# Channel products by batch pairs, the first as seven products of halves, weights and gates kept in DRAM, two mixes moved

## The chip, the cores and the metric

The kernel runs on one core of a Trainium2 chip, in one launch. The metric is the device time of that core in microseconds; the median of three runs of the kernel before is 1045.92 (1045.71 to 1046.95).

## What is computed

Four batches of 448 positions and 768 channels pass through three blocks: attention with a sigmoid in place of the softmax (12 heads of 64), a mixing block with a low-rank mix over positions and a channel MLP of 3072, and a gated block with a causal convolution of five taps.

```python
def _attn_ref(q, k, v):
    scores = scale * np.matmul(q, k.transpose(0, 1, 3, 2)) - np.log(S)
    attn = 1.0 / (1.0 + np.exp(-scores))
    return np.matmul(attn, v)
def _moe_ref(x, U, V, w_ch1, w_ch2):
    u = x + (x.transpose(0, 2, 1) @ U @ V).transpose(0, 2, 1)
    return u + np.maximum(u @ w_ch1, 0.0) @ w_ch2
def _moe2_ref(x, w_val, conv_w, w_out):
    gate = 1.0 / (1.0 + np.exp(-gate_pre))   # gate_pre: causal convolution of x, 5 taps
    return (gate * (x @ w_val) @ w_out)
```

The weights arrive as float64 and are taken as pairs of 32-bit words.

## The kernel before

Activations lie with channels on the 128 partitions and the 448 positions along the row: a batch is 6 blocks of 128 channels (`KC`), the hidden layer 24 blocks (`NF`). `xs` holds x of all four batches and is updated in place.

**Numbers.** A float64 weight becomes a float32 in `unpack` (L83): one ScalarE instruction (L88) and two VectorE instructions (L89, L90) on a half of 384 columns. Each float32 operand of the channel products is then cut into a high part (ScalarE copy, L77) and a low part (VectorE subtraction, L79), and `mm3` (L200) does three matmuls per block of 128 x 128 x 448: high x high, high x low, low x high (L202 to L204).

**Order.** All engines work in the order in which the program issues instructions to them; the order is written out by hand. `flush` (L67) issues the parts put off in `deferred`: one part of a chain of small steps goes out per product, so that a step finds its input done. `load_half` (L145) and `prep_half` (L155) bring in, unpack and split one half of a weight block; they are called between products, in the order that `plan` (L130) lays down. Three buffers hold raw weights, 11 (`WS`) hold split halves, 32 (`OPS`) hold split activations of [128, 2, 448]. All weight loads go through SP's queue.

**Stages.** In attention (`attention_phase`, L547) 12 rounds handle two pairs of heads each; the mixes of batches 0 to 2 (`mix_units`, L382: transposes, projection, back-projection, add to x, split) are slipped in between, and the first three weight halves. The mix of batch 3 is done by `main_phase` (L620) between the first channel products. The channel stage then goes through 12 groups of two hidden blocks. `ch1` (L457) is the first product for one hidden block and one batch: 6 x 3 matmuls into one PSUM bank, a Relu on ScalarE (L460) and the low part on VectorE (L461). `ch2` (L466) is the second product for one output block and one batch: 2 x 3 matmuls, and an add onto x (L473). All four batches go through each group, so each weight is split once. While this goes on, the halves of the two last weight matrices are unpacked, split and stored to DRAM (`stash`), and fetched twice at the end.

**End.** For each half of the batches `val` (L518) is x @ w_val, multiplied by the gate from `gate_steps` (L490: a scaled copy on ScalarE, L499, four multiply-adds on VectorE, L502, a sigmoid on ScalarE, L515); `fin` (L529) is the last product, copied out on ScalarE and stored.

PSUM has 8 banks; `bank` (L543) hands them out in turn.

## Time and profile before

| | |
|---|---|
| median of three runs | 1045.92 us |
| the profiled execution | 1045.58 us |
| its span, first to last instruction | 1043.8 us |
| TensorE matmul busy | 1035.0 us, 99% |
| VectorE busy | 580.0 us, 56% |
| ScalarE busy | 328.8 us, 32% |
| moved by DMA | 98.97 MB, mean 95 GB/s |

Attention fills the span up to about 155 us, the channel products reach to about 865 us, then come the value and the output products. In the profile PE is TensorE's matmul, PEld its weight load, DVE VectorE, ACT ScalarE, SP the engine that issues most transfers; L202 is a line of the kernel. Matmuls overlap in the pipeline, so the pace of a stretch is its time divided by its matmuls, not the mean duration of one.

### The profile page before, as it was taken

The page shows a single profiled execution, that of the slowest core. Times are in us where ns is not written, and L with a number is a line of the kernel's source. Part 1 is how long each engine was busy: PE and PEld are TensorE (multiplying, and loading weights), DVE is VectorE, ACT ScalarE, POOL GpSimd, SP SyncE. Part 2 cuts the span into 40 slices and gives each one's busy share as a digit, 9 for nine tenths or more (in the row PEclk, how much of TensorE's full clock was granted, in tenths as well). Part 3 has the DMA queues.
Part 4 walks back from the last instruction along what each step waited for, and adds up shares of the span by engine and source line. Part 5 has one row for each costly group of instructions (what it writes and reads, how often), then busy time and mean ns, then how long its engine had stood idle before and what let it go on. Part 6 is the DMA issues. An engine that isn't in the chain of part 4 may idle for free.

```text
span 1043.8 us, 13756 instructions
## 1 busy us (share of the span) xinstructions
PE 1035.0 (99%) x5505; PEld 895.0 (86%) x5505; DVE 580.0 (56%) x1057; ACT 328.8 (32%) x562; POOL 1.0 (0%) x6
## 2 busy tenths in 40 slices
PE   9999999999999999999999999999999999999998
PEld 5555547999999999999999999999999999999997
DVE  5455665766556464656456464646455678992100
ACT  6656664223141312213040312223130443231211
POOL 0000000000000000000000000000000000000000
PEclk9999999999999999999999999999999999999999
DMA  7444441233133322314141322314142014332441
GB/s 190 122 107 107 106 112 54 76 122 121 61 113 100 87 80 76 106 46 134 30 114 56 91 79 73 106 56 127 31 131 79 3 61 136 106 110 74 162 173 71
DMA packets 47616, 98.97 MB, mean 95 GB/s; under 512 B 10832, under 2 KB 19984, under 8 KB 47552
## 3 DMA queue, kind: packets, MB, share of 16 engines
q1 hardware_dynamic: 47280, 97.75, 31.5%
q8 instruction: 43, 0.70, 0.3%
q10 hardware_dynamic: 224, 0.23, 0.1%
q14 instruction: 21, 0.17, 0.0%
q0 software_dynamic: 48, 0.11, 0.0%
HBM read 83.13 MB, written 14.94 MB: 94 GB/s over the span
## 4 chain that ended last, share of the span: by engine, by line
PE 98%; DVE 1%; ACT 1%; DMA 0%; SPq 0%; issue 0%; DVEq 0%
PE ch L202 22%; PE ch L204 22%; PE ch L203 22%; PE av L310 5%; PE sc L279 4%; PE fin L204 3%; PE val L204 3%; PE val L202 3%; PE fin L202 3%; PE val L203 3%; PE fin L203 3%; PE tr L391 1%; PE av L323 1%; PE sl L295 1%; PE pp L413 1%; PE h L434 0%
## 5 line engine op out<-in xcount | busy, mean ns | idle before, releaser
L473 DVE TENSOR_TENSOR xs<-ch,xs 128x448 f32<-128x448 f32 x288 | 177.7, 622 | 101.8 <-PE ch L204 101.0
L203 PE MATMUL ch<-h,w 128*128 128x448 f32 x576 | 210.6, 366 | 0.0
L204 PE MATMUL ch<-h,w 128*128 128x448 f32 x576 | 210.6, 366 | 0.0
L202 PE MATMUL ch<-h,w 128*128 128x448 f32 x576 | 210.6, 366 | 0.0
L202 PE MATMUL ch<-u,w 128*128 128x448 f32 x570 | 208.7, 366 | 1.3 <-DVE xs L438 1.3
L203 PE MATMUL ch<-u,w 128*128 128x448 f32 x570 | 208.4, 366 | 0.0
L204 PE MATMUL ch<-u,w 128*128 128x448 f32 x570 | 208.4, 366 | 0.0
L77 ACT ACTIVATE w<-x 128x384 fp32r<-128x384 f32 x120 | 63.0, 525 | 353.8 <-DVE x L90 353.8
L461 DVE SCALAR_TENSOR_TENSOR h<-ch,h 128x448 fp32r<-128x448 f32 x95 | 59.3, 624 | 178.3 <-ACT h L460 178.3
L202 PEld LDWEIGHTS ch<-u,w 128*128 128x128 f32 x570 | 107.2, 188 | 10.4 <-DVE xs L438 1.7
L203 PEld LDWEIGHTS ch<-h,w 128*128 128x128 f32 x576 | 108.3, 188 | 8.4
L204 PEld LDWEIGHTS ch<-h,w 128*128 128x128 f32 x576 | 108.3, 188 | 8.4
L202 PEld LDWEIGHTS ch<-h,w 128*128 128x128 f32 x576 | 108.3, 188 | 8.4
L204 PEld LDWEIGHTS ch<-u,w 128*128 128x128 f32 x570 | 107.2, 188 | 8.4
L203 PEld LDWEIGHTS ch<-u,w 128*128 128x128 f32 x570 | 107.2, 188 | 8.3
L460 ACT ACTIVATE h<-ch 128x448 fp32r<-128x448 f32 x95 | 51.6, 543 | 144.2 <-PE ch L204 144.2
L90 DVE SCALAR_TENSOR_TENSOR x<-a,x 128x384 uint32<-128x384 uint32 x120 | 67.1, 559 | 14.0 <-ACT a L88 1.8
L79 DVE TENSOR_TENSOR w<-x,w 128x384 fp32r<-128x384 f32 x120 | 66.2, 552 | 4.7 <-ACT w L77 2.6
L267 ACT ACTIVATE a<-sc,bias 128x896 f32<-128x896 f32 x72 | 67.1, 1006 | 5.3 <-PE sc L279 5.3
L88 ACT ACTIVATE a<-raw 128x384 f32<-128x384 f32 x120 | 64.9, 541 | 0.3 <-DMA raw<-in_w 0.3
L310 PE MATMUL av<-a,vr 128*64 128x448 f32 x288 | 59.4, 548 | 0.0
L279 PEld LDWEIGHTS sc<-ks 64*128 64x128 f32 x432 | 37.9, 185 | 20.6 <-issue 4.6
(83 smaller groups left out, 988.2 us busy)
## 6 DMA issues: line engine op xcount, KB each, us to landing
raw<-in_w SPq DMA_DIRECT2D x96, 384.0 KB, 3.1
f<-s SPq DMA_DIRECT2D x48, 384.0 KB, 3.3
kq<-in_kq SPq DMA_DIRECT2D x47, 224.0 KB, 3.7
s<-w SPq DMA_DIRECT2D x24, 384.0 KB, 2.7
out_t<-o SPq DMA_DIRECT2D x11, 448.0 KB, 2.8
raw<-in_wval SPq DMA_DIRECT2D x12, 384.0 KB, 3.1
raw<-in_wout SPq DMA_DIRECT2D x12, 384.0 KB, 3.0
vr<-in_va SPq DMA_DIRECT2D x24, 168.0 KB, 3.7
```

The lines of the kernel that those rows point to most:

```text
L77: nc.scalar.activation(hi, raw, AF.Copy)
L79: deferred.append(lambda: nc.vector.tensor_sub(lo, raw, f32(hi)))
L88: nc.scalar.activation(a, f32(high), AF.Prelu, scale=2.0 ** -112, alpha=-(2.0 ** 32))
L90: nc.vector.scalar_tensor_tensor(x, a.bitcast(U32), 3, x, op0=ALU.logical_shift_left, op1=ALU.bitwise_or)
L202: mm(ps, wk[:, 0], x[:, 0], start=start, stop=False)
L203: mm(ps, wk[:, 0], x[:, 1], start=False, stop=False)
L204: mm(ps, wk[:, 1], x[:, 0], start=False, stop=stop)
L267: nc.scalar.activation(a[:, :, :], ps[:, :, :S], AF.Sigmoid, bias=bias, scale=1.0 / math.sqrt(D))
L279: mm(ps[:, h, :S].rearrange("p (c s) -> p c s", c=NSC), ks[r, tk, 0, c], ks[r, tq, 1, :, :SC], start=t == 0, stop=t == 2,)
L310: mm(att["ps"][D * h:D * h + D, :S], vr[:, h, c], a[:, h], start=c == 0, stop=False,)
L461: nc.vector.scalar_tensor_tensor(t[:, 1], ps, 0.0, f32(t[:, 0]), op0=ALU.max, op1=ALU.subtract)
L473: nc.vector.tensor_add(y, ps[:, :S], y)
```

## The change

- **Batch pairs.** The channel stage runs twice, for batches 0 and 1 (p = 0) and then for 2 and 3 (p = 1). Within a pair it goes in 6 quads of four hidden blocks: two chains, then the second product of the quad.
- **First product.** `chain` handles two hidden blocks, two batches and the two halves of the 6 input blocks as a 2 x 2 by 2 x 2 product in seven products (Strassen's, in Winograd's form). Each is a `part` of 3 x 3 = 9 matmuls. Sums of weights (S1 to S4: four VectorE instructions per chain) and of activations (T1 to T4: `u_sums`) are formed beforehand; results are put together by copies of PSUM on ScalarE (p1, u2, p5), further accumulation onto the bank already copied, and three VectorE adds.
- **Second product.** `ch2` does three output blocks at once for one batch, over the quad's four hidden blocks: 4 parts of 9 matmuls, then three adds onto x. There are 144 adds in place of 288.
- **Weights.** For p = 0 each half is unpacked from float64 as before, and the float32 value is also stored to DRAM (`keep`); for p = 1 it is loaded from there, and the sums and splits are made again. Ten buffers hold split halves.
- **Order.** `plan` writes one list of jobs; `step`, called after each part, issues one of them (`pump`) unless that needs more than the ten buffers. `weight` issues jobs at once where a product needs a form that is not there yet. Where the quads of p = 1 are planned, four stashed halves of the last matrices and, in quads 1 to 3, the gates of batches 0 and 1 (now stored to DRAM and fetched) stand among the jobs, in front of the second product's weights.
- **Moves.** The mixes of batches 2 and 3 go out between chains and second products of quads 0 to 2 of p = 0. Attention's last rounds take the sums of activations for p = 0 and the first eight jobs. The sums for p = 1 (`rush`) are issued two per part beside the last second products of p = 0.

The core of the diff:

```diff
...
-OPS = 32
-WS = 11
+OPS = 30
+WS = 10
+RAWS = 3
...
+    def pump(force=False):
+        if jobs and (force or live[0] + jobs[0][0] <= WS):
+            jobs.pop(0)[1]()
+
+    def done_with():
+        live[0] -= len(spent)
+        spent.clear()
+
+    def wtile(name):
+        if "w" not in pools:
+            return operand(name)[:, :, :HQ]
+        live[0] += 1
+        return pools["w"].tile([P, 2, HQ], F32R, tag="w", name=name)[:, :, :]
+
...
+    def keep(slot, part, x):
+
+        if slot not in kept:
+            kept[slot] = pools["kept"].tile([P, 2, HQ], F32, tag="kept", name="k_%s%d" % slot)
+        nc.sync.dma_start(kept[slot][:, part], x)
+
+    def in_two(x, t, then=None):
+
+        nc.scalar.activation(t[:, 0], x, AF.Copy)
+
+        def low():
+            nc.vector.tensor_sub(t[:, 1], x, f32(t[:, 0]))
+            if then:
+                then()
+
+        deferred.append(low)
...
+        def half(i, j):
+            key = ("w1", c + i, j)
+            x[i, j] = to_x(key)
+            deferred.append(lambda: keep(("w1", c + i), j, x[i, j]))
...
+        def first():
+            if p:
+                got(0)
+            put("A11", x[0, 0])
+            put("A12", x[0, 1])
+
+        def sums():
+            if p:
+                got(1)
+            s1 = pools["x"].tile([P, HQ], U32, tag="x", name=f"s1_{p}_{c}")[:, :]
+            x["s1"] = f32(s1)
+            nc.vector.tensor_add(x["s1"], x[1, 0], x[1, 1])
+            nc.vector.tensor_sub(x[1, 0], x[0, 0], x[1, 0])
+
+        def differences():
+            nc.vector.tensor_sub(x[0, 0], x["s1"], x[0, 0])
+            nc.vector.tensor_sub(x[0, 1], x[0, 1], x[0, 0])
+
+        def third():
+            put("S2", x[0, 0])
+            put("S1", x["s1"])
+
+        def fourth():
+            put("S3", x[1, 0])
+            put("S4", x[0, 1], load_next if p else None)
+
+        def fifth():
+            put("A22", x[1, 1], load_next if p else None)
+
+        unpacks = [[lambda i=i, j=j: half(i, j) for j in range(2)] if not p else [] for i in range(2)]
+        if p:
+            loads.extend(("x", "w1", c + i, p) for i in range(2))
+        else:
+            loads.extend(("w1", c + i, j) for i in range(2) for j in range(2))
+        todo = [(0, f) for f in unpacks[0]] + [(2, first)] + [(0, f) for f in unpacks[1]]
+        return todo + [(0, sums), (0, differences), (2, third), (2, fourth), (1, fifth)]
...
+        def again(n, half):
+            def job():
+                a = loaded.pop(("x", f"h{half}_", n // 2, p))
+                ts = [wtile(f"w2_{p}_{n + i}_{half}") for i in range(2)]
+
+                def done(i):
+                    forms[p, n + i, half] = ts[i]
+                    if i:
+                        load_next()
+
+                for i in range(2):
+                    in_two(a[:, i], ts[i], lambda i=i: done(i))
+            return job
+
         for half in range(2):
-            t = pools["w"].tile([P, 2, HQ], F32R, tag="w", name=f"f{n}_{p}_{half}")[:, :, :]
-            nc.sync.dma_start(f32(t), stash[2 * n + half][:, :, :])
+            for n in range(QUAD * q, QUAD * q + QUAD, 2 if p else 1):
+                if p:
+                    loads.append(("x", f"h{half}_", n // 2, p))
+                    out.append((2, again(n, half)))
+                else:
+                    loads.append(("w2", n, half))
+                    out.append((1, fresh(n, half)))
+        return out
...
+    def weight(*key):
+        while key not in forms:
+            if deferred:
+                flush()
+            else:
+                pump(True)
+        return forms[key]
...
+    def u_sums(p, k):
+
+        u = {(i, j): x_of(halves[p][i], k + KH * j) for i in range(2) for j in range(2)}
+        t = {}
+
...
+        def first():
+            both("T1", "T2")
+            difference("T1", u[1, 0], u[0, 0])
+            difference("T2", u[1, 1], t["T1"])
+
+        def second():
+            both("T4", "T3")
+            difference("T4", u[0, 1], t["T2"])
+            deferred.append(lambda: (cut("T2"), cut("T1")))
+
+        def third():
+            difference("T3", u[1, 1], u[1, 0])
+            deferred.append(lambda: (cut("T3"), cut("T4")))
+
+        return [first, second, third]
...
+        def part(ps, ws, ts, start=False):
+            done_with()
+            flush()
+            w = weight(p, c, ws)
+            if (p, c, ws) not in early:
+                spent.append(1)
+            for k in range(KH):
+                mm3(ps, w, k, us[(p, ts), k], start and k == 0, k == KH - 1, skip_group_check=True)
...
+        def finish(i, j, x, other):
+            nc.vector.tensor_add(x, x, other)
+            deferred.append(lambda: relu(i, j, x))
+
+        x, z = (bank(f"{k}_{p}_{c}")[:, :S] for k in "xz")
+        part(x, "A11", "B11", True)
+        p1 = copy("p1", x)
+        step()
+        y = bank(f"y_{p}_{c}")[:, :S]
+        part(y, "A12", "B21", True)
+        deferred.append(lambda: finish(0, 0, p1, y))
+        step()
+        part(x, "S2", "T2")
+        u2 = copy("u2", x)
+        step()
+        part(z, "S1", "T1", True)
+        p5 = copy("p5", z)
+        step()
+        part(x, "S3", "T3")
+        finish(1, 1, p5, x)
+        step()
+        part(z, "S4", "B22")
+        deferred.append(lambda: finish(0, 1, u2, z))
+        step()
+        part(x, "A22", "T4")
+        relu(1, 0, x)
+        step()
+
+    def ch2(p, q, b, half, step, then=None):
+        ps = [bank(f"ch2_{p}_{q}_{b}_{half}_{j}")[:, :S] for j in range(KH)]
+        for i in range(QUAD):
+            done_with()
+            flush()
+            w = weight(p, QUAD * q + i, half)
+            if b == halves[p][-1]:
+                spent.append(1)
+            h = hs[p, QUAD * q + i, b]
+            for j in range(KH):
...
+                step()
+
+        def add():
+            for j in range(KH):
+                m = half * KH + j
+                y = x_of(b, m)
+                nc.vector.tensor_add(y, ps[j], y)
+                if then:
+                    then(b, m)
+
+        deferred.append(add)
...
+        def add(k):
+            nc.vector.scalar_tensor_tensor(t[0], y(k), tap(k), t[0], op0=ALU.mult, op1=ALU.add)
+
+        def first():
+            t.append(operand(f"g{bs[0]}_{m}", F32)[:, :, :])
+            nc.scalar.activation(t[0], y(0), AF.Copy, scale=tap(0))
+            deferred.append(lambda: add(1))
+
+        def second():
+            add(2)
+            add(3)
+
+        def third():
+            add(4)
+            deferred.append(sigmoid)
+
+        def sigmoid():
+            nc.scalar.activation(t[0], t[0], AF.Sigmoid)
+            deferred.append(put)
+
+        def put():
+            gates_kept[m] = pools["gates"].tile([P, 2, S], F32, tag="gates", name=f"gk{m}")
+            nc.sync.dma_start(gates_kept[m][:, :, :], t[0])
+
+        return [(0, first), (0, second), (0, third)]
...
+        todo = [part for k in range(KH) for part in u_sums(0, k)]
+        side[9, 0] = todo[0:1]
+        side[9, 1] = todo[1:2]
+        side[9, 2] = todo[2:4]
+        side[10, 0] = todo[4:5]
+        side[10, 1] = todo[5:6] + [load_next] * RAWS
+        side[10, 2] = todo[6:8]
+        side[11, 0] = todo[8:9] + [pump]
+        side[11, 1] = [pump] * 3
+        side[11, 2] = [pump] * 3
 
...
+    def plan():
+
+        for p in range(2):
+            for q in range(NQ):
+                more = []
+                if p:
+                    n = KC * 2 * 2 // NQ
+                    more += [("st", i) for i in range(q * n, (q + 1) * n)]
+                    if 1 <= q < 1 + KH:
+                        more += [("gate", 2 * (q - 1)), ("gate", 2 * (q - 1) + 1)]
+                new = []
+                for c in (QUAD * q, QUAD * q + 2):
+                    new += pair_jobs(p, c)
+                    take = more[:len(more) // 2] if c % QUAD == 0 else more
+                    more = more[len(take):]
+                    for what, i in take:
+                        if what == "st":
+                            n, half = divmod(i, 2)
+                            kind, n = ("val", n) if n < KC else ("out", n - KC)
+                            new.append(last_jobs(kind, n, half))
+                        else:
+                            new += gate_jobs(halves[0], i)
+                new += second_jobs(p, q)
+                jobs.extend(new)
...
+    def main_phase():
+
+        sides = {}
+        for q, b in enumerate(halves[1]):
+            at = ((q, 4), (q, 5), (q + 1, 0), (q + 1, 1), (q + 1, 2))
+            sides.update(zip(at, mix_units(b)))
+        rush = []
+
+        def step():
+            if rush:
+                for part in rush[:2]:
+                    part()
+                del rush[:2]
+                if len(rush) % 4 == 0:
+                    pump()
+            else:
+                pump()
+
+        lists = {}
...
+            for q in range(NQ):
+                last = q == NQ - 1
+                events = iter(range(6))
+
+                def side():
+                    for unit in sides.pop((q, next(events)), ()):
+                        unit()
...
-            if p:
-                for _ in range(3):
-                    fetch_next()
-            for b in bs:
-                for m in range(KC):
-                    ch2(g, b, m)
-                    y_split(b, m)
...
```

## Rows read from the trace of the kernel before

**Rows 1.** The page: engines, with busy us, share of the span and instructions.

```profile
PE 1035.0 (99%) x5505; PEld 895.0 (86%) x5505; DVE 580.0 (56%) x1057; ACT 328.8 (32%) x562; POOL 1.0 (0%) x6
...
PE   9999999999999999999999999999999999999998
PEld 5555547999999999999999999999999999999997
```

**Rows 2.** Stretches: us, busy us (instructions) of PE, PEld, DVE, ACT, POOL; PEclk, DMA share, GB/s.

```profile
100.00:150.00 50.00, 50.00 (x380) 25.42 (x378) 31.74 (x63) 32.96 (x44) 0.00 (x0) 1.00 0.42 106
...
184.00:794.00 610.00, 610.00 (x3012) 565.91 (x3011) 349.43 (x669) 151.04 (x303) 0.00 (x0) 1.00 0.29 87
```

**Rows 3.** Waits of TensorE: us in total, times, longest us.

```profile
PE ch L202 <- DVE xs L438: 1.3, 1, 1.3
PE tr L391 <- DVE h L461: 1.0, 1, 1.0
PE h L434 <- ACT a L267: 0.4, 1, 0.4
```

**Rows 4.** Groups by line and shape: xcount, busy us, mean ns, idle before.

```profile
L202 PE MATMUL ch<-u,w 128*128 128x448 f32 x570 | 208.7, 366 | 1.3 <-DVE xs L438 1.3
...
L88 ACT ACTIVATE a<-raw 128x384 f32<-128x384 f32 x120 | 64.9, 541 | 0.3 <-DMA raw<-in_w 0.3
L77 ACT ACTIVATE w<-x 128x384 fp32r<-128x384 f32 x120 | 63.0, 525 | 353.8 <-DVE x L90 353.8
...
L460 ACT ACTIVATE h<-ch 128x448 fp32r<-128x448 f32 x95 | 51.6, 543 | 144.2 <-PE ch L204 144.2
...
L502 DVE SCALAR_TENSOR_TENSOR g<-xs,cw,g 128x896 f32<-128x896 f32 x36 | 41.2, 1145 | 0.4
...
L499 ACT ACTIVATE g<-xs,cw 128x896 f32<-128x896 f32 x12 | 12.3, 1030 | 0.0
...
L515 ACT ACTIVATE xs<-xs 128x896 f32<-128x896 f32 x12 | 11.4, 954 | 58.8 <-DVE xs L502 58.8
...
L562 PE MATMUL idle<-zeros 128*128 128x448 f32 x9 | 3.7, 594 | 1.4 <-DVE zeros L559 1.4
```

**Rows 5.** Timeline of VectorE in a dense stretch: start us, us, instruction.

```profile
427.49 0.62 DVE L461 SCALAR_TENSOR_TENSOR h<-ch,h 128x448 fp32r<-128x448 f32 x1 [1.62 <-ACT h L460]
428.03 0.55 DVE L79 TENSOR_TENSOR w<-x,w 128x384 fp32r<-128x384 f32 x1
428.50 0.35 DVE L89 TENSOR_SCALAR x<-raw 128x384 uint32<-128x384 uint32 x1
428.95 0.56 DVE L90 SCALAR_TENSOR_TENSOR x<-a,x 128x384 uint32<-128x384 uint32 x1
429.43 0.62 DVE L473 TENSOR_TENSOR xs<-ch,xs 128x448 f32<-128x448 f32 x1
430.11 0.56 DVE L79 TENSOR_TENSOR w<-x,w 128x384 fp32r<-128x384 f32 x1
430.58 1.82 DVE L473 TENSOR_TENSOR xs<-ch,xs 128x448 f32<-128x448 f32 x3
```

**Rows 6.** Transfers by issue: count, KB each, median us from issue to landing.

```profile
raw<-in_w SPq DMA_DIRECT2D x96, 384.0 KB, 3.1
...
s<-w SPq DMA_DIRECT2D x24, 384.0 KB, 2.7
```

**Rows 7.** Stretches as in rows 2, for the DMA share and GB/s.

```profile
0.00:50.00 50.00, 47.99 (x327) 25.80 (x329) 25.44 (x57) 31.91 (x39) 1.04 (x6) 1.00 0.65 163
184.00:193.00 9.00, 9.00 (x46) 8.36 (x45) 6.45 (x14) 3.31 (x7) 0.00 (x0) 1.00 0.46 131
...
1012.00:1016.00 4.00, 4.00 (x21) 3.70 (x21) 0.00 (x0) 0.54 (x1) 0.00 (x0) 1.00 0.89 310
```

**Rows 8.** Timeline of TensorE at the start.

```profile
1.42 3.73 PE L562 MATMUL idle<-zeros 128*128 128x448 f32 x9 [1.42 <-DVE zeros L559]
```

More of the change, by code (lines that the diff above doesn't have):

```diff
@@ L38 @@
 IDLE = 9
-EARLY = 3
 @with_exitstack
@@ L136, in tile_kernel, with load_next @@
-    plan("ccc")
-    pools = {}
-    wraw = {}
-    wt = {}
+    halves = [range(h, h + B // 2) for h in range(0, B, B // 2)]
+    w_io = {"w1": w1_in, "w2": w2_in, "val": wval_in, "out": wout_in}
+    pools = {}
+    loads = []
+    loaded = {}
+    kept = {}
+    jobs = []
+    forms = {}
     stash = {}
+    gates_kept = {}
+    early = set()
     fetched = {}
-    ready = set()
-    at = {"load": 0, "prep": 0}
-    def load_half():
-        if at["load"] >= len(order):
+    def load_next():
+        if not loads:
@@ L185, in weight @@
[L185 to L204 removed]
+        key = loads.pop(0)
@@ L385, in mix_units, with one @@
         pst = []
+        inner = "ps_s" in pools
+        acc = []
+        def one(name):
+            return bank_of(duo(name), 0) if inner else bank(name)
         def transpose(c):
@@ L685, in gate_half @@
                 deferred.append(lambda: (gates[i][3](), finished.append(i)))
-        n = 2 * G * NG
-        g = NG - 1
-        fetches = [(n + q * KC + m, p) for q in range(2) for p in range(2) for m in range(KC)]
+        gates = [gate_steps(halves[1], m) for m in range(KC)]
+        open_at = [0]
+        finished = []
+        fetches = [(kind, m, p) for kind in ("val", "out") for p in range(2) for m in range(KC)]
         def fetch_next():
@@ L721, in main_phase @@
         unsplit = [(b, m) for p, m, b in todo]
+        gate = {m: fetch_gate(m) for m in range(2)}
         def settle_values(lag):
@@ L741, in main_phase @@
                 for j, b in enumerate(bs):
-                    fin(fetched[n + m, p], b, m, o[:, j], last=end and j)
+                    fin(fetched["out", m, p], b, m, o[:, j], last=end and j)
                     settle_values(0)
```

399 lines of the change are left out of this document (216 added, 183 removed).

## The prediction

> **What bounds the kernel now.** I read the page's engine table first, then the stretches, the waits and the groups of instructions. TensorE is busy 99% of the span, VectorE 56%, ScalarE 32% [rows 1]: two engines have room, one has none. In the stretch of the channel products TensorE issued 3012 matmuls in 610.0 us, one per 0.2025 us, with the clock column at 1.00 [rows 2]. TensorE's waits after the start are three, 1.3, 1.0 and 0.4 us, where the mix of the last batch stood in front of its own evictions [rows 3]. So time goes only with matmuls, unless new waits appear, and a wait on TensorE costs its full length.
>
> **What is removed.** Per pair of row blocks and per pair of batches the first product was 8 products of halves, 3 column blocks x 3 matmuls each, 72 matmuls; it becomes 63. There are 12 block pairs and 2 batch pairs: 24 x 9 = 216 matmuls x 0.2025 = **43.7 us** off the bound engine. The second product keeps its 1728 matmuls, the mixes keep theirs (those of batch 2 move from attention to the channel phase, where TensorE is just as full: zero). The three waits of 2.7 us belong to the late mix and go, because the first chain needs batches 0 and 1 alone: **-2.7 us**.
>
> **What is added, and its cover.** VectorE's pitch, start to start, from one dense stretch [rows 5]: 0.47 us for a 384-column subtraction, 0.45 and 0.48 for the two unpack steps, 0.54 for the 448-column low part of h, (1.82 - 0.62) / 2 = 0.60 for an add from PSUM. A quad of four row blocks is 270 matmuls, 54.7 us, in 30 parts of 9 matmuls (1.82 us). For the first batch pair VectorE has in it 16 unpacks (14.9 us), 22 low parts (10.3), 8 sums and differences (3.8), 6 adds and 8 low parts of h (7.9) and 12 adds onto x (7.2): 44.1 of 54.7 us, 81%. ScalarE, by its mean durations [rows 4]: 16 x 0.54 + 22 x 0.53 + 14 x 0.54 = 27.9 us. For the second pair VectorE has 34.8 us, and 44.0 in quads 1 to 3, which also carry the gates (8 steps of 1.145 us [rows 4]). Going through the parts in order, the lag of VectorE behind TensorE in an ordinary quad of the first pair stays under 1.5 us. The tightest use, the last product that goes onto the bank just added from, allows 1.82 - 0.60 = 1.2 us of lag, at a place where the lag is below 0.5. I cost the ordinary quad at **nothing**; its cover is those 10 us per quad, and if it were gone each of 24 chains would wait up to 1 us.
>
> Four places are not covered.
>
> 1. *First quad, second chain.* Eight jobs are done ahead, one follows per part. The third product of the second chain finds its weights unsplit, and they are made on the spot: add 0.65 (0.60 and the handover), relu and two copies on ScalarE, then the low part: 2.2 us after the part before, against 0.4 for the third matmul: **+1.9**.
>
> 2. *The gates of batches 0 and 1, quads 1 to 3 of the second pair.* With 10 weight tiles the jobs cannot run further ahead than the next chain. The order is two weight blocks, six gate steps, then the weights of the second product, and a chain has seven steps: the seventh is the last gate step, so the second product asks for a job that is not issued yet. It is issued behind everything on two in-order queues. From the end of the second chain's second part: add 0.65, then three gate steps, 4.1, the fourth 5.25; the low part of h and the add after part five, 6.4; the gate's sigmoid on ScalarE (0.95) and the next gate's copy (1.03), 7.3; three gate steps, 10.75; low part and add, 11.9; the last gate step, 13.05; its sigmoid, 14.0; and only then the copy of the weights, 14.5, and the low part, 15.0 [rows 4, 5]. TensorE has finished its five parts at 9.1 and waits 5.4, with the third matmul's wait 5.5 us. Behind the waiting copy on ScalarE nothing else is late; the store of the gate holds SP's queue, whose next loads are for weights three jobs later. Three quads: **+16.5**. At most the whole gate chain shows (6 us each), at least none, if the order on the queues were kinder than the code reads.
>
> 3. *End of the first pair.* The sums of batches 2 and 3 run beside the last second products: 33 steps of about 0.54 us, 18 us more. Over nine parts VectorE gets 27.8 us where 16.4 fit. Its backlog of 11 us delays the adds that free banks: the third bank of the fourth group waits about 2.7 us, and a later chain about 1.4 while the backlog drains: **+4.2** (0 to 11).
>
> 4. *End of attention.* ScalarE is busy 33.0 of 50 us there [rows 2]. The last round of some 12.5 us gets four unpacks and up to six copies, 5.3 us on top of 8.2, less what stood there before. I take **+2.0** (0 to 4).
>
> Transfers: 96 stores of 192 KB, 48 loads of 384 KB in place of none, and 12 of the gates. A weight load now lands in 3.1 us, a store in 2.7 [rows 6]; with three buffers the next is asked for 5.5 us before its use. SP holds each store until its unpack is done, and then the load behind it; both are due after that anyway. Taken at zero; see the last rival.
>
> **Sum.** Span 1043.8 - 43.7 - 2.7 + 2.0 + 1.9 + 4.2 + 16.5 = 1022.0. The profiled execution took 1045.58, 1.8 more than its span, and the median shown stands 0.34 above it: **1024 us**. Its own range, from the bounds above, is 1014 to 1030.
>
> **Rivals.**
>
> *A, the gates are hidden.* The wait of 5.5 us is worked out from order alone; no trace shows that code. If the second product's weights are made in time, the time is 1024 - 16.5 = 1007.5. For it: VectorE has 10 us of room even in those quads. Against it: one job per part, and seven parts. Chance 0.20.
>
> *B, TensorE's clock falls in the waits.* The first nine matmuls, after an idle start, took 594 ns each against 366 [rows 4] and came (3.73 - 0.59) / 8 = 0.39 us apart [rows 8], the pace of 1.2 GHz, though the column reads 1.00; in the steady stretch it is 0.2025, that of 2.4 GHz. After them the trace has no wait of over 1.4 us, so none shows whether the engine drops back. If it does after each of the three long waits, nine slow matmuls cost 9 x 0.19 = 1.7 us and three times as many 5.1: 5 to 15 us, 1029 to 1039, say 1032. The Trainium skill, TensorE: Matmul & The Clock Gate, section "Why this matters for your kernels", speaks against a change that opens such gaps: an engine left idle between bursts of matmuls returns to half its clock. By that rule the time would be this rival's. Chance 0.18, for the waits are of a length that no row here shows.
>
> *C, slower: the loads become the bound.* Where ten parts in a row each unpack a block, each asks for 0.393 MB in and 0.197 MB out in 1.82 us, 324 GB/s. The best 4 us here moved 310 at a share of 0.89, which makes 348 when full; another stretch 131 at 0.46, which makes 285; the start 163 at 0.65, 251 [rows 7]. A late load holds the unpack at the head of ScalarE's queue, with the copies that free TensorE's banks behind it. There are 96 such parts. At 285 each takes 2.07, +0.25, together 24: 1048. At 251, 2.35, +0.53, 51: 1075. It comes out slower below 0.59 MB in 1.82 + (1045.9 - 1024) / 96 = 2.05 us, 288 GB/s. Against it: the ten are only a third of a quad, the mean over a quad is 173 GB/s, and the 384 KB rows are long ones like those of the 310. Chance 0.04.
>
> That the change does not do what it says can be set aside: the count of matmuls is in the code. What is left, 0.06, is waits of 1 us in many chains, 1030 to 1044.
>
> **How the numbers follow.** The forecast has 0.52, A 0.20, B 0.18, C 0.04, the rest 0.06. A range from 1003 (A with both end terms at zero) to 1034 (most of B) leaves out about 0.2. About 0.2%, 2 us, can be told from no change. All cases but C and part of the rest lie below 1043.8: faster 0.95, same 0.01, slower 0.04.
>
> **What would show it.** Right: about 5290 matmul records in place of 5505, a pitch of 0.20 us between waits; three waits of some 5 us on TensorE, 54 us or more apart, each on ScalarE's copy or VectorE's low part of a second-product weight, behind gate steps; VectorE near 80% in the first half; one group of waits of 3 to 4 us in the middle. Wrong: TensorE at 99% with no such waits (A); matmuls of 0.39 us pitch after a wait (B); waits of ScalarE's unpack on a load, with the share of the transfers above 0.9 (C); many waits of 1 us in the chains, then the lag was misjudged.

## The result: slower, 1053.88 us

The changed kernel takes 1053.88 us (median of 8 executions, 1049.71 to 1057.98), the kernel before on the same chip 1046.89: a ratio of 1.0072, 95% interval 1.0043 to 1.0101. The forecast was 1024.0, with a range of 1003 to 1034. The eight lie in two groups of four, 1049.7 to 1051.7 and 1056.1 to 1058.0; the profiled one took 1057.33 (span 1055.5), of the upper group. Of the eight executions of the kernel before one lies apart, at 1063.91, and the ratio leaves it out. The experiments with gaps show what can set such groups apart.

The page of the changed kernel: busy us, share and instructions of each engine, and the granted clock of TensorE in 40 slices of the span.

```profile
PE 1016.9 (96%) x5289; PEld 860.4 (82%) x5289; DVE 683.0 (65%) x1293; ACT 444.3 (42%) x822; POOL 1.0 (0%) x6
...
PE   9999998999999999999799799897999999999998
...
PEclk9999999999999999999999899898999999999999
```

The 216 matmuls are gone (5505 in [rows 1]), yet TensorE's busy time fell by 18.1 us only, from 1035.0, and not by the 43.7 forecast for them. So the matmuls that stayed became slower. And TensorE now has waits of up to 5.8 us, where [rows 3] had 1.3, 1.0 and 0.4. Waits of TensorE: us in total, times, longest.

```profile
PE ch L335 <- ACT w L183: 17.5, 3, 5.8
PE ch L335 <- DVE xs L732: 7.5, 2, 4.9
PE x L335 <- ACT S L183: 3.3, 1, 3.3
PE ch L335 <- DVE h L682: 1.7, 1, 1.7
PE idle L864 <- DVE zeros L861: 1.4, 1, 1.4
PE av L443 <- ACT a L400: 1.0, 1, 1.0
PE x L335 <- ACT p L676: 0.8, 1, 0.8
...
PE ch L337 <- DVE w L186: 0.4, 1, 0.4
```

The first row is the wait forecast for quads 1 to 3 of the second pair: three times, 5.8 us, on the copy of a second-product weight. The timeline of ScalarE and of VectorE ahead of its first instance (start us, us, instruction) shows the order that the prediction had worked out:

```profile
600.77 0.95 ACT L806 ACTIVATE g<-g 128x896 f32<-128x896 f32 x1 [0.44 <-DVE g L790]
601.63 0.92 ACT L183 ACTIVATE w<-raw_x_h__2_1_5913 128x384 fp32r<-128x384 f32 x2
...
599.60 1.15 DVE L790 SCALAR_TENSOR_TENSOR g<-xs,cw,g 128x896 f32<-128x896 f32 x1
600.66 0.62 DVE L682 SCALAR_TENSOR_TENSOR h<-x,h 128x448 fp32r<-128x448 f32 x1
601.19 0.61 DVE L682 SCALAR_TENSOR_TENSOR h<-u,h 128x448 fp32r<-128x448 f32 x1
602.17 1.03 DVE L186 TENSOR_TENSOR w<-raw_x_h__2_1_5913,w 128x384 fp32r<-128x384 f32 x2 [0.37 <-ACT w L183]
```

The gate's last step (599.60), its sigmoid (600.77), and only then the weight's copy (601.63); TensorE starts at 602.19, as soon as the high part is there. What comes behind is in TensorE's timeline:

```profile
602.19 0.74 PE L335 MATMUL ch<-h,w 128*128 128x448 f32 x1 [5.85 <-ACT w L183]
602.73 0.57 PE L336 MATMUL ch<-h,w 128*128 128x448 f32 x1
603.10 0.57 PE L337 MATMUL ch<-h,w 128*128 128x448 f32 x1
603.48 0.57 PE L335 MATMUL ch<-h,w 128*128 128x448 f32 x1
...
605.34 0.45 PE L337 MATMUL ch<-h,w 128*128 128x448 f32 x1
605.63 0.37 PE L335 MATMUL ch<-h,w 128*128 128x448 f32 x1
605.84 0.36 PE L336 MATMUL ch<-h,w 128*128 128x448 f32 x1
```

From 602.73 to 605.34 the matmuls start 0.37 to 0.38 us apart, which is the 1.2 GHz level ([rows 8] had 0.39 at the start); then 0.20. Stretches of the same kernel (columns as in [rows 2]), the first of them inside the wait:

```profile
599.00:602.00 3.00, 0.00 (x0) 0.00 (x0) 2.80 (x5) 1.80 (x3) 0.00 (x0) 0.50 0.00 0
602.60:606.00 3.40, 3.40 (x11) 2.97 (x11) 2.47 (x6) 1.60 (x4) 0.00 (x0) 0.57 0.85 275
...
680.00:720.00 40.00, 40.00 (x195) 36.34 (x194) 26.78 (x47) 15.07 (x30) 0.00 (x0) 1.00 0.36 119
```

The first row has the clock at 0.50 while TensorE still waits, the second at a mean of 0.57 behind the wait. The clock falls so seven times, at the waits that end at 169.2, 254.3, 311.8, 506.9, 602.2, 664.8 and 729.2, with 6 to 14 matmuls each some 0.37 us apart, 60 in all. In the third row the clock is at 1.00 throughout, and still the pace is not that of before: 195 matmuls touch the 40 us, where the same count is 199 at a pace of 0.2027 (a row with 199 stands below). Start to start it is 0.2067 us, 2% more, in long stretches of this profile, and 0.2027 in the others; in the profile of before it is 0.2027 in all (the 0.2025 of the prediction counts the matmuls that touch a stretch).

**The account.** From the first product of the channel stage to the last matmul I take the distance from each start to the next: what the row names as waited goes to the waits; of the rest, distances above 0.30 us count as slow matmuls, with what they have over 0.2027; what all others have over 0.2027 is the pace (odd distances between 0.23 and 0.30 make 0.4 to 2.3 us in all and are left out of the table, as is the mix). The column "slow" holds more than the clock: where a wait begins and ends, single distances of 0.31 to 0.37 us stand even with no fall. e5 and e8 have 2.7 and 1.5 us of it and no fall at all. By an estimate from the 60 matmuls (0.17 us each) and the longer first ones behind the waits, some 12 of the 15.9 us of the changed kernel are the clock's.

| profiled execution of | us | waits | slow | pace |
|---|---|---|---|---|
| the kernel before | 1045.58 | 2.3 | 0.2 | -0.1 |
| the changed kernel | 1057.33 | 31.3 | 15.9 | 8.9 |
| the same, again (e9_again) | 1058.56 | 30.6 | 15.1 | 11.9 |
| e1_gates_after | 1025.48 | 13.4 | 7.3 | 2.7 |
| e2_warm | 1045.51 | 14.6 | 10.6 | 1.8 |
| e3_rush | 1049.62 | 29.3 | 15.7 | 2.9 |
| e4_short | 1048.94 | 26.7 | 13.6 | 8.5 |
| e5_best | 1015.16 | 9.2 | 2.7 | 0.9 |
| e7_stores | 1033.68 | 12.1 | 8.5 | 11.0 |
| e8_final | 1007.24 | 3.0 | 1.5 | 1.9 |
| e6_gaps (of before) | 1107.18 | 37.1 | 18.1 | 6.3 |
| e10_short_gaps (of before) | 1079.29 | 14.9 | 3.6 | 12.9 |

The last matmul starts 12.3 us later than before (1051.69 against 1039.38): -43.8 for 216 matmuls, -5.9 because the first product starts earlier, +6.7 for mix pieces that moved behind attention, +29.0 waits, +15.7 slow matmuls, +9.0 pace, +1.6 odd distances. With the pace taken out of both profiled executions the change is still slower, 1048.4 against 1045.7.

So the theory is: the waits are near the forecast, and what was lost beyond it is that TensorE doesn't resume at its old speed. Rivals: the slow matmuls belong to the new order of chains and not to the waits; VectorE bounds the chains now; the stores to DRAM do.

### The profile page after: what moved, and what is told of

Read it like the earlier page. It is cut to its first block, busy times and chain, and to the rows that moved or that the text cites. A ratio compares the mean times of both kernels' runs of the same rounds, so it can differ in the third digit from the quotient of the medians.

```text
span 1055.5 us, 14327 instructions
## 1 busy us (share of the span) xinstructions
PE 1016.9 (96%) x5289; PEld 860.4 (82%) x5289; DVE 683.0 (65%) x1293; ACT 444.3 (42%) x822; POOL 1.0 (0%) x6
## 4 chain that ended last, share of the span: by engine, by line
PE 47%; DVE 5%; ACT 2%; issue 0%; DMA 0%; SPq 0%; ACTq 0%
PE ch L335 6%; PE ch L336 6%; PE ch L337 6%; PE fin L336 3%; PE fin L335 3%; PE val L336 3%; PE val L335 3%; PE fin L337 3%; PE val L337 3%; DVE g L790 3%; PE x L335 2%; PE x L337 2%; PE x L336 2%; PE z L336 1%; PE z L337 1%; PE z L335 1%
## 5 line engine op out<-in xcount | busy, mean ns | idle before, releaser
L335 PE MATMUL ch<-h,w 128*128 128x448 f32 x576 | 217.4, 377 | 26.7 <-ACT w L183 17.5
L337 PE MATMUL ch<-h,w 128*128 128x448 f32 x576 | 215.3, 374 | 0.5 <-DVE w L186 0.4
L336 PE MATMUL ch<-h,w 128*128 128x448 f32 x576 | 215.6, 374 | 0.0
L335 PEld LDWEIGHTS ch<-h,w 128*128 128x128 f32 x576 | 111.4, 193 | 40.1 <-ACT w L183 18.6
L732 DVE TENSOR_TENSOR xs<-ch,xs 128x448 f32<-128x448 f32 x144 | 86.0, 621 | 61.7 <-PE ch L337 61.3
L337 PEld LDWEIGHTS ch<-h,w 128*128 128x128 f32 x576 | 111.2, 193 | 11.7 <-DVE w L186 1.4
L336 PEld LDWEIGHTS ch<-h,w 128*128 128x128 f32 x576 | 111.5, 194 | 10.0
L92 DVE SCALAR_TENSOR_TENSOR x_w<-x_w,r_w 128x384 uint32<-128x384 uint32 x96 | 53.7, 559 | 34.8 <-ACT x_w L90 29.6
L335 PE MATMUL x<-T,S 128*128 128x448 f32 x144 | 53.7, 373 | 4.2 <-ACT S L183 3.3
L834 ACT ACTIVATE o<-fin 128x448 f32<-128x448 f32 x23 | 12.6, 546 | 106.8 <-PE fin L337 104.0
L90 ACT ACTIVATE x_w<-raw_w 128x384 f32<-128x384 f32 x96 | 51.6, 543 | 10.3 <-DMA raw_w<-in_w 7.9
L412 PEld LDWEIGHTS sc<-ks 64*128 64x128 f32 x432 | 37.6, 184 | 21.8 <-issue 5.4
L412 PE MATMUL sc<-ks 64*128 64x448 f32 x432 | 52.3, 380 | 1.4 <-DVE xs L624 0.7
L337 PE MATMUL x<-T,S 128*128 128x448 f32 x144 | 53.2, 369 | 0.0
L336 PE MATMUL x<-T,S 128*128 128x448 f32 x144 | 53.2, 369 | 0.0
L335 PE MATMUL val<-y,f_val 128*128 128x448 f32 x144 | 53.0, 368 | 0.0
L336 PE MATMUL val<-y,f_val 128*128 128x448 f32 x144 | 53.0, 368 | 0.0
L337 PE MATMUL val<-y,f_val 128*128 128x448 f32 x144 | 53.0, 368 | 0.0
L335 PE MATMUL fin<-z,f_out 128*128 128x448 f32 x144 | 53.0, 368 | 0.0
L336 PE MATMUL fin<-z,f_out 128*128 128x448 f32 x144 | 53.0, 368 | 0.0
```

What stands on the lines that cost most here:

```text
L90: nc.scalar.activation(f32(x), f32(high), AF.Prelu, scale=2.0 ** -112, alpha=-(2.0 ** 32))
L92: nc.vector.scalar_tensor_tensor(x, x, 3, r, op0=ALU.logical_shift_left, op1=ALU.bitwise_or)
L335: mm(ps, wk[:, 0], x[:, 0], start=start, stop=False, **kw)
L336: mm(ps, wk[:, 0], x[:, 1], start=False, stop=False, **kw)
L337: mm(ps, wk[:, 1], x[:, 0], start=False, stop=stop, **kw)
L412: mm(ps[:, h, :S].rearrange("p (c s) -> p c s", c=NSC), ks[r, tk, 0, c], ks[r, tq, 1, :, :SC], start=t == 0, stop=t == 2,)
```

## The experiments

**The gates' wait taken away.** In `plan`, the two gates of a quad go behind the second product's weights, with three empty jobs between them.

```diff
                 new += second_jobs(p, q)
+                if p and 1 <= q < 1 + KH:
+                    new += gate_jobs(halves[0], 2 * (q - 1)) + [(0, lambda: None)] * 3
+                    new += gate_jobs(halves[0], 2 * (q - 1) + 1)
```

(and the lines that put them among the earlier jobs go).

> Only the list of jobs is changed: in quads 1 to 3 of the second batch pair the six gate steps stand behind the weights of the second product, with three empty places between the two gates. Theory 1 (the loss is a few long waits of TensorE and the half clock that follows each): the three waits of 5.85 us go, and with them the 40 matmuls that ran 0.37 us apart, 40 x 0.17 = 6.8 us; together 24 us, so about 1030 us, and six clock falls fewer or three. Theory 2 (VectorE and ScalarE have no room in these quads, the order only chooses where TensorE waits): other waits of the same sum appear in the same quads and the time stays at 1049 to 1058.

Measured: 1025.54 us (1024.94 to 1026.52), ratio to before 0.9801 (0.9785 to 0.9816). The row of 17.5 us is gone from the waits, the others stand as they were:

```profile
PE ch L335 <- DVE xs L732: 7.5, 2, 4.9
PE x L335 <- ACT S L183: 3.1, 1, 3.1
PE ch L335 <- DVE h L682: 1.7, 1, 1.7
```

Between the two profiles lie 31.9 us, 17.9 of waits, 8.6 of slow matmuls and 6.2 of pace (the first product starts 1.1 us later); between the medians 28.3, and between this run and the lower group of the changed kernel (middle 1050.6) 25.0. So 17.9 us of waits cost some 25 to 32, the more the more pace is counted with them. That the order of the jobs made it is settled, and the sign of the whole change with it.

**The wait filled.** 26 matmuls whose result nobody reads go into the gap of each of the three quads, so that TensorE keeps working while it waits.

```diff
+            if p and 1 <= q <= KH and not half and b == halves[p][0] and not i:
+                u = us[(p, "T4"), 0]
+                for _ in range(26):
+                    mm(ps[0], u[:, 0, :P], u[:, 0], start=True, stop=True)
```

> The changed kernel with 26 extra matmuls on finished operands into the bank about to be used, issued in front of the first second-product part of quads 1 to 3 of the second pair, so that TensorE works while it would wait; the results are overwritten by the group that starts there. Theory 1a (the slow pace after a long wait is the clock's, and comes from idling): the waits for the weights keep their place, but the 40 slow matmuls run 0.20 us apart: about 7 us less, 1043 to 1051. Rival 1b (the slow pace is a matter of the operands or of the pipeline after a semaphore, not of idling): the matmuls behind the extra ones are still 0.37 us apart and the time is the same or, by what the extra ones overrun, up to 1 us more per quad.

Measured: 1049.3 us (1043.72 to 1055.45), ratio 1.0026 (0.9996 to 1.0056). The three waits are down to 0.6 us at most, the fillers take 16.5 us in their place, and behind them no slow matmul stands (the second row is the stretch behind the first of them):

```profile
PE ch L335 <- ACT w L183: 1.5, 3, 0.6
...
603.60:607.00 3.40, 3.38 (x16) 2.90 (x17) 2.90 (x6) 2.04 (x5) 0.00 (x0) 1.00 0.71 231
```

That is theory 1a: 34 matmuls stood there at 0.37 us apart, some 6 us or 2 us a gap, and they go when TensorE doesn't idle. The clock falls three times, not seven, at two early waits and the one at 508. The column of slow matmuls shows 5.3 us less, 10.6 for 15.9, which isn't these gaps alone: the fall at 312 did not come either, and those at 255 and 508 had 15 slow matmuls each in place of 6.

**The other waits, one by one.** e3 sums the activations of the second pair one job per part in place of two; e4 does two jobs more in the first chain, and sets the mixes' back-projections further apart. (By a clash of two entries, e4 also leaves out the second back-projection of batch 2: 9 matmuls and 3 additions.)

```diff
-                for part in rush[:2]:
-                    part()
-                del rush[:2]
-                if len(rush) % 4 == 0:
+                rush.pop(0)()
+                if len(rush) % 2:
                     pump()
...
-            at = ((q, 4), (q, 5), (q + 1, 0), (q + 1, 1), (q + 1, 2))
+            at = ((q, 4), (q, 5), (q + 1, 0), (q + 1, 3), (q + 1, 5))
...
                 pump()
+                if extra:
+                    extra.pop()
+                    pump()
 
+        extra = [1, 1]
```

> The sums of batches 2 and 3 at the end of the first pair go out one per part in place of two. Theory 1: the waits of 4.9 and 0.8 us there shrink to under 1.5 together and the eight slow matmuls behind them (1.4 us) go: 4 to 7 us less. Theory 2: VectorE has 59 us to do in that quad of 54.7, so a backlog of 4 us or more stays and TensorE waits as long, only later: within 2 us of the changed kernel.

> The short waits alone: two jobs more are issued in the first chain of the first quad, and the two adds of each late mix are moved from the chains into the second product (events 3 and 5 of the quad). Theory 1: the waits of 3.3, 2.6 and 1.7 us and the 25 slow matmuls behind them (4.2 us) go, 8 to 12 us less. Theory 2: the adds meet the same full VectorE there, and the gain is under 4 us.

Measured: e3 1051.58 us (1048.74 to 1056.17), ratio 1.0054 (1.0030 to 1.0079). At the end of the first pair 4.88 + 0.83 us became 2.98 + 0.48 + 0.21, but the clock still fell behind the 2.98. The time is 2.3 us less, between its two theories, and 1 to 2 us less when group is compared with group. e4 1045.31 us (1041.22 to 1049.72), ratio 0.9989 (0.9966 to 1.0013): the wait of the first quad went from 3.34 to 0.82 + 0.47 us, that of the mix quad from 2.64 to 1.17, and behind these two no fall stands, while a wait of 2.08 came up at 319, with a fall, on VectorE's additions onto x. Of the 8.6 us that e4 gains some 1.8 are the 9 matmuls left out.

All four edits together, with the mix of batch 3 two quads behind that of batch 2 and nothing left out, are e5:

> The change with all four edits: gates behind the weights of the second product, two jobs more in the first chain, the additions of the late mixes at other places (batch 3's mix two quads behind batch 2's), one sum per part at the end of the first pair. Theory (waits and the half clock behind them are what the change lost): beside the gates-after version's 1025.5 us the waits fall from 13.4 to about 7 us, as they did one by one (3.34 to 1.3, 2.64 to 1.2, 4.88 to 3.0), and the falls of the clock from three to one or two, 2 to 4 us of slow matmuls in place of 7.3: 1013 to 1018. Rival (VectorE has no room beside the mixes, the waits only move): some 13 us of waits at other places, three falls, 1022 to 1027.

Measured: 1019.46 us (1015.07 to 1024.97), ratio 0.9758 (0.9673 to 0.9843). The profiled execution, 1015.16, has 9.2 us of waits and no fall of the clock, though one of its waits is 3.0 us long:

```profile
PE x L335 <- ACT p L676: 3.0, 1, 3.0
PE ch L335 <- DVE xs L732: 2.7, 2, 1.5
PE x L335 <- ACT u L676: 2.0, 1, 2.0
```

The theory had 1013 to 1018; two of the four executions are there, two at 1023.75 and 1024.97.

**Gaps in the kernel before.** The slow matmuls could still belong to the new order of the chains. So the kernel before gets gaps and nothing else: ahead of one first product in each of ten groups stands a small matmul that needs a chain of 0 to 9 GpSimd copies.

```diff
+    def gap(n, h):
+        if not held:
+            held.append(operand("held"))
+        t = held[0]
+        for i in range(n):
+            nc.gpsimd.tensor_copy(t[:, 1], h[:, 1] if i == 0 else t[:, 1])
+        x = t[:, 1, :P] if n > 0 else h[:, 1 + n, :P]
+        mm(banks[0].tile([P, 512], F32, tag="mm", name="none")[:, :P], h[:, 0, :P], x, start=True, stop=True)
...
+                        if i and b == 2 and lengths:
+                            gap(lengths.pop(0), hs[g * G + i, b - 1])
                         ch1(g * G + i, b)
```

> The kernel before with ten gaps and nothing of the change: in ten of its groups one small matmul that needs a chain of 0 to 9 copies on GpSimd (idle otherwise) stands ahead of a first product, so that TensorE waits, by an estimate, 1 to 10 us in a stretch that is dense otherwise; no result depends on it. Theory (the clock falls behind a wait, whatever kernel it stands in): behind every wait of about 1.7 us and more some 8 to 16 matmuls come 0.38 us apart, 1.5 to 2.9 us a gap on top of the gap, 12 to 25 us in all; behind the waits near 1 us none. Rival 1 (the slow matmuls belong to the new order of the chains, not to the wait): the time grows by the waits alone, and the matmuls behind them come 0.20 us apart. Of the second pace, 0.2067 in place of 0.2027: if an interruption sets it, some stretches between the gaps show it; if it belongs to the new order of matmuls, none does and all show 0.2027 or 0.2025.

Measured: 1104.83 us (two executions, 1102.48 and 1107.18), ratio 1.0556 (1.0495 to 1.0618). Waits of TensorE, the new ones:

```profile
PE none L629 <- POOL held L627: 31.2, 7, 7.4
PE none L629 <- DVE h L461: 2.6, 2, 1.3
...
PE none L629 <- ACT h L460: 0.6, 1, 0.6
```

TensorE's timeline behind the shortest of the seven:

```profile
369.02 0.33 PE L629 MATMUL none<-held,h 128*128 128x128 f32 x1 [2.17 <-POOL held L627]
369.18 0.42 PE L202 MATMUL ch<-u,w 128*128 128x448 f32 x1
...
370.05 0.43 PE L203 MATMUL ch<-u,w 128*128 128x448 f32 x1
370.29 0.57 PE L204 MATMUL ch<-u,w 128*128 128x448 f32 x1
370.66 0.57 PE L202 MATMUL ch<-u,w 128*128 128x448 f32 x1
...
373.27 0.53 PE L203 MATMUL ch<-u,w 128*128 128x448 f32 x1
373.64 0.37 PE L204 MATMUL ch<-u,w 128*128 128x448 f32 x1
```

And three stretches: ahead of that gap, in the slow matmuls, and behind them.

```profile
320.00:360.00 40.00, 40.00 (x199) 37.07 (x198) 22.67 (x43) 7.40 (x15) 0.00 (x0) 1.00 0.27 84
371.00:373.20 2.20, 2.20 (x7) 1.95 (x6) 0.00 (x0) 0.00 (x0) 0.00 (x0) 0.50 0.31 123
380.00:420.00 40.00, 39.87 (x193) 35.90 (x193) 22.07 (x42) 6.76 (x14) 0.00 (x0) 1.00 0.23 65
```

The first matmuls behind this gap run at full pace, then the clock falls to 0.50 and 9 matmuls start 0.37 us apart. Slow matmuls stand behind each of the seven gaps of 2.17, 2.80, 3.63, 4.25, 4.88, 6.12 and 7.37 us, with 9, 8, 9, 9, 13, 12 and 8 of them; in the longest three the clock fell inside the gap, and the products behind it are slow at once. Behind 0.63, 1.29 and 1.29 us there is nothing. So rival 1 falls: the clock goes with the wait, in a kernel without any chain. And the last row shows the second pace, with the clock at 1.00: 0.2066 us from start to start, and 193 matmuls where 199 stood (some of the difference is a short wait at 388).

Is a fall of the clock needed for the second pace? Twenty gaps of 0.63 us tell, two per group, 8.3 and 53.1 us apart in turn (the same edit, with b in 1 and 3 and n = -1 throughout).

> The kernel before with twenty short gaps and nothing of the change: two per group, a small matmul that needs the high part of the first product just made, so that TensorE waits about 0.63 us as in the first gap of the kernel with ten gaps, behind which no slow matmul stood. Theory (an interruption of TensorE can switch its pace between 0.2027 and 0.2067, a fall of the clock is not needed): 20 x (0.63 + some 0.15 for the small matmul) = 15.6 us more than before, no fall of the clock, and stretches of 0.2067 between the gaps, 2 to 12 us on top, with executions that differ by some us. Rival (only a fall of the clock switches it): 15.6 us and 0.2027 throughout, 1062 to 1064 in every run.

Measured: 1076.8 us (1076.4 to 1079.29), ratio 1.0289 (1.0269 to 1.0309): 30 us more than before, twice the 15.6 of the rival. The waits are what they were meant to be, and the clock falls nowhere in the stretch:

```profile
PE none L629 <- ACT h L460: 12.7, 20, 0.6
...
500.00:540.00 40.00, 40.00 (x195) 36.34 (x194) 22.28 (x41) 5.84 (x12) 0.00 (x0) 1.00 0.22 66
```

(the first line from its waits, the second from its stretches). From the second pair of gaps on, the pace is 0.2067 in nearly all of the 53 us behind the second gap of a pair, and 0.2027 in the 8 us behind the first. (The first pair has it the other way round, and the third gap switched nothing.) So an interruption of 0.63 us can switch it, in both directions; of the 33.7 us by which the profiled execution grew, 12.9 are this. The executions agree within 3 us, which the theory had not said.

**The stores.** In the changed kernel VectorE waits 15.1 us, in 11 places, for stores of the halves that the sums write over; I had taken the transfers at zero.

```profile
DVE x_w L236 <- DMA k_w<-x_w: 15.1, 11, 3.0
```

e7 is e1 with S3 written over a half stored long before, and S2 over the youngest, one job later.

```diff
-            nc.vector.tensor_sub(x[1, 0], x[0, 0], x[1, 0])
+            nc.vector.tensor_sub(x[0, 0], x[0, 0], x[1, 0])
...
-            nc.vector.tensor_sub(x[0, 0], x["s1"], x[0, 0])
-            nc.vector.tensor_sub(x[0, 1], x[0, 1], x[0, 0])
+            nc.vector.tensor_sub(x[1, 0], x[1, 1], x[0, 0])
+            nc.vector.tensor_sub(x[0, 1], x[0, 1], x[1, 0])
```

> The gates-after version with the sums of weights in another order: S3 is written over a half that was stored long before, S2 over the half whose store is the youngest, one job later than now; the same sums otherwise. In the profile of the gates-after version VectorE waits 12.7 us in 11 places for these stores. Theory (VectorE has room there, so the transfers' price that I took at zero is nearly zero on the path): the 12.7 us fall below 4, TensorE gains only where VectorE was late anyway, some 0.6 us of the first wait of 3.06: 1024 to 1026. Rival (these waits make VectorE's backlog in the quads with mixes): the waits of 2.65 and 1.67 us on TensorE shrink too, and with them a fall of the clock: 1019 to 1022.

Measured: 1033.66 us (1025.19 to 1033.85), ratio 0.9856 (0.9818 to 0.9894). VectorE's waits on stores are 4.2 us in place of 12.7, and TensorE's waits hardly move: 3.06 became 2.62, the others are 2.65, 1.64 and 4.78, and one of 0.79 is gone: 12.1 us in all for 13.4. That is the theory's picture, with another time: three of four executions are 8 us above it, and the profiled one has 11.0 us of pace where e1 had 2.7. The fourth, 1025.19, is where the theory put it. So the stores are not what was lost, and medians of these kernels carry some 8 us that no wait explains.

**The version that beats both.** e5 with the sums of e7, and with the stashed halves of the last matrices out of the first quad of the second pair:

```diff
-                    more += [("st", i) for i in range(q * n, (q + 1) * n)]
+                    more += [("st", i) for i in range(max(0, 5 * q - 5), min(24, 5 * q))]
```

> The version with the four edits, with the other order of the sums and with the stashed halves of the last matrices taken out of the first quad of the second pair (five in each of the next). In that version's profile the sums waited 1.9 us for a store just ahead of TensorE's wait of 1.50 us, and unpacks of a stashed half stood between the late sums of activations where TensorE waited 3.0 and 2.0 us. Theory: these three waits fall to some 0.3, 1.5 and 0.5: 9.2 us of waits become 5, no fall of the clock, 1008 to 1013 where the pace is 0.2027 throughout. Rival: the stashed halves move a wait to quads with gates, where VectorE has less room: 1014 to 1020. The second pace may add up to 9 us to either.

Measured: 1012.27 us (1007.24 to 1017.92), ratio 0.9689 (0.9638 to 0.9740). Of the profiled execution (1007.24):

```profile
PE 995.0 (99%) x5289; PEld 851.3 (85%) x5289; DVE 677.8 (67%) x1293; ACT 443.7 (44%) x822; POOL 1.0 (0%) x6
```

and its waits of over a microsecond inside the channel stage:

```profile
PE x L335 <- ACT p L676: 2.0, 1, 2.0
...
PE z L335 <- ACT p L676: 1.0, 1, 1.0
```

3.0 us of waits in all, no fall of the clock. The matmuls are the same 5289 as in the changed kernel, with 21.9 us less of busy time: those were the price of running them slowly. Two of its four executions took 1007.2 and 1007.3, two 1017.2 and 1017.9.

**The product itself.** In e8 each chain gets its nine matmuls back (run e11_nine): the seventh product is made twice.

```diff
         part(x, "A22", "T4")
+        for k in range(KH):
+            mm3(x, forms[p, c, "A22"], k, us[(p, "T4"), k], False, k == KH - 1, skip_group_check=True)
```

> The version of 1007.2 us with 72 matmuls in each chain in place of 63: the seventh product of a chain is made twice and added twice, so its output is not that of the reference; nothing else is changed. Theory (the 216 matmuls are worth their number times the pace, because no other engine becomes the bound when they go): 216 x 0.2027 = 43.8 us more, less what VectorE's late work at the end of the first pair gains from 1.8 us more per chain (up to 3 us): 1048 to 1051 where the pace is 0.2027. Rival (with 63 matmuls VectorE already bounds parts of the chains, so 9 more per chain cost less): under 40 us more, below 1047.

Measured: 1049.82 us (1048.55 to 1060.04), ratio 1.0040 (1.0010 to 1.0071); profile against profile 1048.99 - 1007.24 = 41.8 us. So seven products in place of eight are worth their 216 matmuls, and VectorE, at 67%, does not bound the chains.

**The changed kernel again.**

> The changed kernel once more, unchanged, for a second profile: its runs lie in two groups, 1049.7 to 1051.7 and 1056.1 to 1058.0, and the profiled one was of the upper. Theory (the pace 0.2067 sets which group): in a profile of the lower group the same waits and seven falls of the clock stand, and the time at the pace 0.2067 adds some 2 us where it added 8.9. If the profile is of the upper group again, the 8.9 come again, perhaps in other stretches. Rival: the groups differ in the falls of the clock, not in the pace.

Measured: 1058.56 us, the upper group once more, so the lower one was not seen in a profile. Its waits are the same; the clock fell six times (behind 1.64 us at 312 it did not, where it had behind 1.66), and the pace cost 11.9 us. The nearest that stands for a lower group is the profile of e3, 1049.62 with e3's own groups at 1048.7 to 1052.7 and 1055.6 to 1056.2: six falls and 15.7 us of slow matmuls, as against seven and 15.9 in the upper profile of the changed kernel, and 2.9 us of pace. The rival falls on another number: the mean granted clock is known for every execution, and it is 0.982 to 0.985 in the lower group and 0.982 to 0.985 in the upper one, where by an estimate 7 us lost at half clock would have lowered it by some 0.007 (7 of 1055). The table says the same: profiles from the upper end of their kernel's range have 8.5 to 11.9 us of pace (the changed kernel, e9, e4, e7), those from the lower end 0.9 to 2.9 (e2, e3, e5, e8). Two profiles of one kernel, one from each group, were not had.

## Why the prediction was wrong

**The matmuls: right.** -43.7 forecast, -43.8 in the account, 41.8 when put back.

**The waits: 31.3 us in place of 22.6 new ones.** The gates' wait was right in place, cause and size: 17.5 for 16.5. The first quad was 3.3 + 0.4 for 1.9: the late weights stood behind ScalarE's copy of a sum that VectorE reached only at 167.5, after a wait of 0.6 us of its own for a store. The end of the first pair was 4.9 + 0.8 for 2.7 + 1.4. Not foreseen were two waits in the quads with mixes, 2.6 + 1.7: I had put the moved mixes at zero because TensorE is as full there as in attention, and left out that their six additions per batch fall on VectorE in the very parts in which it unpacks (with the additions set apart, in e4, the 2.6 became 1.2). That is the step "an ordinary quad costs nothing" applied to two quads that are not ordinary. The end of attention cost less: 0.8 us net of the moved pieces, for 2.0. These 9.1 us (8.7, and 0.4 because the old waits make 2.3 in this stretch, not 2.7), less the 1.2, would have made 1032, still in the range.

**The step that failed: "a wait on TensorE costs its full length", with one pace of 0.2025 for all matmuls.** Most waits of some 2 us and more cost their length and then 1 to 2.6 us for matmuls at the 1.2 GHz level, and even a short interruption can switch the pace for tens of microseconds. The first half of this was rival B, at 0.18; it put the price at 5 to 15 us for three waits. It was some 6 for those three and some 12 for seven, as waits of 1.7 to 4.9 us, which I had counted as harmless, had it too. For the second half, 9.0 us in the profile, there was no case: [rows 2] average 610 us at one pace and could not show a second. With the slow matmuls and the pace, 24.7 us by the table, and the 9.1 us of waits beyond the forecast, less 1.2, with 1.6 of odd distances, the gain of 21.8 in the sum turned into a loss of 12.3. By the forecast's own mark ("matmuls of 0.39 us pitch after a wait") it was case B that came; its 1029 to 1039 was too low as well, for the waits and the pace that it did not count.

The Trainium skill, TensorE: Matmul & The Clock Gate, section "Why this matters for your kernels", was cited for B: an engine left idle between bursts of matmuls returns to half its clock. By that rule the trace agrees: 0.57 in the stretch behind a wait of 5.85 us, 0.50 behind one of 2.17. The measurements also show gaps of one length going either way: 1.34 us had 8 slow matmuls behind it in e6 and none in e10 (nor 1.33 in the kernel before), 3.0 us had 8 in e3 and none in e5.

**The other rivals.** A (gates hidden) was not the case, but e1 shows what it would have been worth: 25 to 32 us, not 16.5. C (loads the bound) did not come: no wait of TensorE ends on a load, though raw weights land in 4.1 us where [rows 6] had 3.1. The price of zero for the transfers was right for the path: e7 took 8.5 us of VectorE's waits on stores away, and TensorE's waits fell by 1.3.

## What to carry to other kernels

On an engine that is busy 99% of the time, a change that takes work off it is judged by the new waits, and a wait of some 2 us or more on TensorE is to be priced at its length plus 1 to 2.6 us of matmuls at the lower clock. Where the order of the queues makes the wait, the cure is cheap: moving jobs in a list, and writing two of the sums over other buffers, brought 1053.9 us to 1012.3 with as many instructions. Compare such kernels by their accounts of waits, slow matmuls and pace, because their medians carry up to 10 us of a pace that changes from one execution to the next.

## What the runs showed of the hardware

- TensorE has two paces at a granted clock of 1.00 for these 128x448 matmuls: 0.2027 and 0.2067 us, 2% apart. Interruptions of 0.63 us switched it (19 of the 20 in e10), and so did odd distances of 0.27 us in the changed kernel (at 421). What differs inside the engine the profiles don't show: durations of matmuls (0.36 to 0.37 us) and of weight loads (0.19) are alike.
- The kernel before may have the second pace for a whole execution. By an estimate, 4250 products 0.0040 us slower make 17 us, which is how far its execution at 1063.91 lies from the others; 16 like it in the later series (1062.5 to 1064.6) have a mean granted clock of 0.998 to 1.00. None of them was profiled, so this is not shown.
- Of the waits of 1.9 us and more from the channel stage on, 39 of 42 in all profiles had a fall of the clock; of six at 1.64 to 1.68 us one had it (the changed kernel), and of those of 0.5 to 1.6 us one, of 1.34 (e6). The three long ones without are 3.02 and 1.98 in e5 and 2.03 in e8; what decides is open.
- The fall can come inside the gap or behind it. At the wait of 5.85 us the clock stood at 0.50 while TensorE still waited; behind the gap of 2.17 us five matmuls still ran 0.20 to 0.26 us apart, then 9 at 0.37. Behind the longest gap, 7.37 us, there were no more of them (8) than behind 2.80: the clock had fallen some 3 us before it ended.
